# Pinning the issue order of three engines in a fused linear-attention and ReGLU kernel

## The chip, the cores and the metric

The kernel runs on one core of one Trainium2 chip. The metric is device time in microseconds (us), the median of several executions. One execution was also taken by the hardware profiler; times inside the kernel, such as "at 43.8 us", count from the start of its span. TensorE does matmuls, VectorE (DVE) and ScalarE (ACT) elementwise work, GpSimd (POOL) a few small operations, and SyncE (SP) issues nearly all DMA.

## The reference

The input `x` has 2048 tokens of 1024 values; weights and activations are bf16.

```python
phi = lambda t: jnp.where(t > 0, t + 1, jnp.exp(t)) + 1e-6
pq, pk = phi(q), phi(k)                      # 32 heads of 32, q, k, v = layernorm(x) @ wqkv
kv = einsum("bhsd,bhse->bhde", pk, v)
z = einsum("bhsd->bhd", pk)
o = einsum("bhqd,bhde->bhqe", pq, kv) / (einsum("bhqd,bhd->bhq", pq, z)[..., None] + 1e-6)
h = x + o.reshape(B, S, D) @ wo
n = layernorm(h)
gate, up = n @ W_gate, n @ W_up              # 1024 -> 3584
out = h + (gate * (gate > 0) * up) @ W_down  # 3584 -> 1024
```

## The kernel before

**Tiling.** Tokens go in 16 tiles of 128. Nearly every large product is done in the Strassen–Winograd way: both operands are split in two by two blocks, sums of blocks are formed (`left_sums` L113–123 for activations: L117 to L120; `right_ops` L127–138 for weights: L133 to L136; `weight_sums` L634–650 for gate and up: L642, L646, L647, L648), seven products replace eight, and their results are combined. Those sums and combinations are VectorE's work. `strassen` (L144–203) is the generator that does one product: matmuls into PSUM banks of tags A (two banks), D (one) and E (two); after products m1, u2 and u3, `snap` (L154) copies a PSUM bank to SBUF on ScalarE, so that TensorE may go on accumulating in the bank; and `fin` combines a bank with a copy.

**Stages.**
- *k and v, 0–122 us.* `ln_T` (L265) takes a token tile, forms its layernorm statistics on VectorE (L272, L275, and L287, which is mean times minus rstd), rstd on ScalarE (L277, L278), and the normalised tile `xn` on ScalarE (L288). The first tiles are transposed by TensorE (`transpose_in`, L299, copied out by L300), the others by a DMA. The first tiles then use plain products (`k_plain`, `v_plain`), later groups of four use `strassen` (`k_unit`, `v_unit`; matmuls L314, combinations L211 for k and L375 for v). phi of a result is finished by an exp on ScalarE (L216) and two operations on VectorE (L217, L218). `kv_tile` (L383) accumulates kv and z.
- *q, 122–206 us.* `q_unit` (L447, matmuls L454), with the same phi.
- *Attention, 146–270 us* (`attn_stages`, L513), in steps by tile with a lag between its parts: numerator and denominator in matmuls `nd` (L527) of 132 columns; 1/denominator on ScalarE as exp(−ln) (L531, L533); their product `o_sb` on VectorE (L534, two buffers); a transposing DMA to `oT` (L541); the `attn` matmuls with wo (L557); the residual sum on VectorE (L560); then the second layernorm (L572, L574–L578) to `hn`, another transposing DMA (L581) and its left sums.
- *Early gate and up products, 205–287 us* (`early_quad` L731, matmuls L738, combinations L747–L752), beside the second half of attention.
- *The rest, from 287 us:* gate and up products (`quad`, matmuls L851, copies L856, combinations L860–L864), then the down projection (L1171, L1345). Here `tc.manual_schedule` (L811) fixes the order of TensorE, VectorE and ScalarE as written.

**What sets the order.** Up to 287 us a scheduler decides in which order each engine's instructions are issued, from priorities (`tc.high_priority`), dependencies and its own estimate of when things are ready; a few edges are added by hand (`tc.issue_after`, and two `tc.add_manual_dep` at L793–798). Each engine then runs its instructions in that fixed order, and an instruction whose input is not there holds what is behind it. DMAs are issued by SyncE in SyncE's own order.

Of the kernel before, what the change touches and what calls it, by code (L numbers as in the profile page):

```python
# [19 lines left out]
def _load_act_set(nc, set_name="natural_log_exp_and_others"):  # L20
    from concourse.act_sets import SETS

    idx = [s.name for s in SETS].index(set_name)
    nc.scalar.add_instruction(
        mybir.InstLoadActFuncSet(
            name=nc.get_next_instruction_name(), act_func_set_id=idx, ins=[], outs=[]
        )
    )


@with_exitstack
def block_kernel(ctx: ExitStack, tc: tile.TileContext, x, wqkv, wo, wg, wu, wd, out, H: int):
    nc = tc.nc
# [19 lines left out]
    assert Dh == 32 and DW == NW and S % (4 * P) == 0 and FC % 4 == 0 and KC % 4 == 0  # L53

    _load_act_set(nc)

    consts = ctx.enter_context(tc.tile_pool(name="consts", bufs=1))
# [163 lines left out]
    order = [(i * HS + s * SW) // P + tt for s in range(NS) for i in range(2) for tt in range(NT)]  # L221
# [573 lines left out]
    for t, copy in ((order[-2], ("m1", 1)), (order[-1], ("u3", 1))):  # L795
        tc.add_manual_dep(squared[t].ins, quad_copies[2][copy].ins.name,
                          mybir.DependencyInfo(mybir.DependencyClass.NoSync, mybir.DependencyReason.DATA),
                          reason="order")
    ectx.close()
    pqctx.close()  # L800
    psctx.close()
# [220 lines left out]
    for r, (wt, f, fi, toks) in enumerate(runs):  # L1022
# [3 lines left out]
        for n, s in enumerate(toks):  # L1026
            first = n == 0 and grouped and fi == 0
# [502 lines left out]
@with_exitstack  # L1530
def kernel(
    ctx: ExitStack,
    tc: tile.TileContext,
    A_x: bass.AP,
    A_wqkv: bass.AP,
    A_wo: bass.AP,
    B_x: bass.AP,
    B_W_gate: bass.AP,
    B_W_up: bass.AP,
    B_W_down: bass.AP,  # L1540
    out: bass.AP,
):
    block_kernel(tc, A_x, A_wqkv, A_wo, B_W_gate, B_W_up, B_W_down, out, H=32)
# [30 lines left out]
```

## Time and profile before

| | us |
|---|---|
| median of 5 runs (lowest, highest) | 735.89 (735.41, 736.92) |
| the profiled execution | 735.41 |
| its span | 733.6 |
| first matmul of the hand-ordered part (accA, L851) | 287.3 |
| TensorE, VectorE, ScalarE busy in the span | 720.4, 580.4, 323.8 |

The span is what the profile covers; 1.8 us of the execution lie around it. In the list of waits a row reads: engine, the tile and line that waited, the engine, tile and line that it waited for, then total us, number of waits and the longest. In a timeline a row reads: start, length, engine, line, operation, tiles, sizes, and in brackets the idle time just before it with what ended that. In a table by stretches of time each engine has its busy us and its number of instructions; the granted TensorE clock (1.00 is full speed), the share of the 16 DMA engines' time that was busy, and GB/s stand last. "A <- B" reads: A is written from B, or A waits for B.

### The profile page before, as it was taken

To read this page: it belongs to the slowest core of one execution; us is meant where nothing else is said; L and a number is where in the kernel's file an instruction comes from. 1 tells how busy PE (TensorE), PEld (TensorE's weight loads), DVE (VectorE), ACT (ScalarE), POOL (GpSimd) and SP (SyncE) were. 2 spreads that over 40 slices of the span, in tenths; PEclk is the share of its full clock that TensorE was granted. 3 is DMA by queue.
4 is the path that set the end of the run, shared out by engine and by line. 5 is a ranking of instruction groups with operands and counts; after the bars stand their busy time and mean duration, and the time that the engine had idled before them with its cause. 6 is when DMAs were issued, how large, how long until landed. Compare 5 with 4: busy or idle time off the path is not lost.

```text
span 733.6 us, 10630 instructions
## 1 busy us (share of the span) xinstructions
PE 720.4 (98%) x4000; PEld 379.6 (52%) x4000; DVE 580.4 (79%) x1039; ACT 323.8 (44%) x580; POOL 20.7 (3%) x56
## 2 busy tenths in 40 slices
PE   7999999999999999999999999999999999999997
PEld 3444555444444444444444444444444468888566
DVE  6997644676789767789998998988987379996677
ACT  4876553778886655444344444444444120000000
POOL 1000000000000000000000000000000001100210
PEclk9999999999999999999999999999999999999999
DMA  9765002169976524177557576565553499977932
GB/s 314 166 150 159 1 1 76 41 150 224 236 167 172 136 73 136 44 226 222 162 169 238 204 231 229 172 201 171 181 179 120 142 396 332 313 258 276 257 45 58
DMA packets 144708, 128.89 MB, mean 176 GB/s; under 512 B 50960, under 2 KB 127888, under 8 KB 144656
## 3 DMA queue, kind: packets, MB, share of 16 engines
q1 hardware_dynamic: 137584, 123.30, 55.5%
q0 software_dynamic: 5312, 3.15, 3.6%
q10 hardware_dynamic: 1760, 1.77, 0.7%
q8 instruction: 31, 0.51, 0.3%
q14 instruction: 21, 0.17, 0.1%
HBM read 76.81 MB, written 39.85 MB: 159 GB/s over the span
## 4 chain that ended last, share of the span: by engine, by line
PE 81%; DVE 8%; DMA 5%; ACT 4%; issue 1%; SPq 0%; DVEq 0%; POOL 0%; ACTq 0%
PE accA L851 21%; PE accA L1345 8%; PE attn L557 6%; PE accX L851 6%; PE accY L851 5%; PE Aq L314 3%; PE Aq L738 3%; PE accA L1171 3%; PE accX L1345 3%; PE Aq L454 3%; PE accY L1345 2%; PE accA L939 2%; PE Eq L314 2%; PE accY L1171 2%; PE accX L1171 2%; PE Eq L738 2%
## 5 line engine op out<-in xcount | busy, mean ns | idle before, releaser
L856 ACT COPY snap<-accA 128x1024 f32<-128x1024 f32 x52 | 52.4, 1010 | 65.9 <-PE accA L851 65.7
L861 ACT ACTIVATE gu<-gu 128x512 bf16<-128x512 bf16 x72 | 45.4, 630 | 80.4 <-DVE gu L860 80.3
L851 PEld LDWEIGHTS <-tg 128*128 128x128 f16 x384 | 37.6, 98 | 45.4 <-issue 0.2
L851 PEld LDWEIGHTS <-tu 128*128 128x128 f16 x384 | 37.6, 98 | 45.3
L557 PE MATMUL attn<-wo_mem,oT 128*128 128x512 bf16 x256 | 58.6, 379 | 1.5 <-DVE o_sb L534 1.3
L851 PE MATMUL accA<-hn,tg 128*128 128x512 f16 (+1 forms) x192 | 49.3, 379 | 0.0
L851 PE MATMUL accA<-hn,tu 128*128 128x512 f16 (+1 forms) x192 | 49.3, 379 | 0.0
L154 ACT COPY u<-Aq 128x512 f32<-128x512 f32 x54 | 31.4, 583 | 36.8 <-PE Aq L314 19.4
L1345 PEld LDWEIGHTS <-x 128*128 128x128 f16 (+1 forms) x448 | 43.8, 98 | 5.5
L557 PEld LDWEIGHTS <-oT 128*128 128x128 bf16 x256 | 24.6, 97 | 31.9 <-issue 3.5
L860 DVE TENSOR_TENSOR gu<-accX,snap 128x1024 bf16<-128x1024 f32 x26 | 31.7, 1219 | 10.2 <-ACT snap L856 7.9
L860 DVE TENSOR_TENSOR gu<-accY,snap 128x1024 bf16<-128x1024 f32 x26 | 31.7, 1218 | 7.7 <-ACT snap L856 7.7
L851 PEld LDWEIGHTS <-wg 128*128 128x128 bf16 x208 | 20.3, 98 | 25.8 <-issue 1.3
L851 PEld LDWEIGHTS <-wu 128*128 128x128 bf16 x208 | 20.4, 98 | 24.5
L314 PEld LDWEIGHTS <-xT 128*128 128x128 bf16 (+1 forms) x192 | 18.6, 98 | 23.7 <-issue 2.3
L534 DVE TENSOR_TENSOR o_sb<-nd,rd 128x384 bf16<-128x384 f32 (+1 forms) x48 | 23.3, 507 | 8.3 <-ACT rd L533 6.1
L1309 POOL DMA_DIRECT2D out_dram<-o x12 | 15.2, 1265 | 505.0 <-DVE o L1305 503.2
L1345 PEld LDWEIGHTS <-xs 128*128 128x128 f16 x280 | 27.4, 98 | 3.2
L560 DVE SCALAR_TENSOR_TENSOR x_res<-attn,x_res 128x512 bf16<-128x512 f32 x32 | 21.9, 686 | 8.6 <-PE attn L557 8.4
L1351 DVE TENSOR_TENSOR snap<-accA,u 128x1024 f32<-128x1024 f32 x16 | 19.5, 1220 | 11.5 <-PE accA L1345 11.4
L864 DVE TENSOR_TENSOR hq<-gu 128x512 bf16<-128x512 bf16 x48 | 20.2, 421 | 10.0 <-ACT gu L861 9.8
L1171 PEld LDWEIGHTS <-x 128*128 128x128 bf16 (+1 forms) x168 | 16.4, 98 | 19.6
(268 smaller groups left out, 1508.8 us busy)
## 6 DMA issues: line engine op xcount, KB each, us to landing
x<-x_dram SPq DMA_DIRECT2D x17, 896.0 KB, 8.7
x_dram<-hq SPq DMA_DIRECT2D x28, 512.0 KB, 3.0
wg<-in_B_W_gate_dram SPq DMA_DIRECT2D x14, 512.0 KB, 4.6
wu<-in_B_W_up_dram SPq DMA_DIRECT2D x14, 512.0 KB, 5.9
x_dram<-hq SPq DMA_DIRECT2D x28, 256.0 KB, 2.4
wraw<-in_B_W_down_dram SPq DMA_DIRECT2D x14, 512.0 KB, 4.2
t_dram<-wt SPq DMA_DIRECT2D x21, 256.0 KB, 2.2
xd<-x_dram SPq DMA_DIRECT2D x6, 896.0 KB, 7.0
```

The costliest lines, as they stand in the source:

```text
L154: copies[nm, v] = nc.scalar.copy(out=snaps[nm, v], in_=bank[v][:])
L314: nc.tensor.matmul(ps[:], lhsT=left[m - 1][:, kc, r + v * P:r + (v + 1) * P], rhs=right[m - 1][:, kc, :], start=(start and kc == 0), stop= ...
L454: nc.tensor.matmul(ps[:], lhsT=rq[m - 1][:, kc, (c + v) * P:(c + v + 1) * P], rhs=left[m - 1][:, kc, :], start=(start and kc == 0), stop=( ...
L534: nc.vector.tensor_tensor(out=ov[:, c0:c0 + n], in0=ndv[:, :, 0:P].rearrange("p k (h e) -> p k h e", h=HPC), in1=rd[:, 0:n, :].unsqueeze(3 ...
L557: nc.tensor.matmul(ps[:], lhsT=st["oT"][:, c, :], rhs=wo_sb[:, c, j * NW:(j + 1) * NW], start=(c == 0), stop=(c == KC - 1))
L738: nc.tensor.matmul(ps[:], lhsT=w(v, m)[:, kc, :], rhs=left[m - 1][:, kc, :], start=(start and kc == 0), stop=(kc == KH - 1), skip_group_ch ...
L851: nc.tensor.matmul(ps[:, v, :], lhsT=w[v][n - 1][:, kc, :], rhs=left[n - 1][:, kc, :], start=(t is not None and kc == 0), stop=(kc == KH - ...
L856: nc.scalar.copy(out=st[nm][:], in_=halves(st["A"]))
L860: add(out=g[:], in0=halves(st[nm]), in1=st[base][:], op=ALU.add)
L861: nc.scalar.activation(out=g[:, 0, :], in_=g[:, 0, :], func=ACT.Relu)
L1171: nc.tensor.matmul(ps[:, t * NW:(t + 1) * NW], lhsT=x_tile(n, s, kh)[:, f, (t0 + t) * P:(t0 + t + 1) * P], rhs=w_tile(n, kh)[:, f, :], sta ...
L1345: nc.tensor.matmul(pv[:, tt, :], lhsT=left(m)[:, f, tt * P:(tt + 1) * P], rhs=right(m)[:, f, :], start=(t is not None and f == 0 and tt % ...
```

## The change

The kernel gets a table, `ISSUE_ORDER`, with one entry for each engine, and a loop at the end of the early gate/up stage. The loop collects the instructions of each engine that were emitted so far, in program order; the table's words ("start*length", a run of program-order numbers) say in which order they shall be issued; and between each instruction and the next in that order an edge of class `NoSync` is added. Such an edge binds the scheduler and adds neither a semaphore nor an instruction.

The order of issue that follows was listed for both kernels, engine by engine. The instructions are the same, and so are the orders of SyncE and GpSimd. TensorE's order differs in 30 places, VectorE's in 54, ScalarE's in 26, nearly all of them one or a few instructions moved past a few others, and none after 287 us. The moves that are spoken of below, by the time at which TensorE started the matmul concerned in the profile before:

| at us | what is moved |
|---|---|
| 16.6–20.2 | L287 of the third tile ahead of two L272 and a sum; L300 and an L288 (ahead of the exp L349) forward |
| 40.5–49.8 | copies L154 and a v copy ahead of the L288 that they followed; L211 ahead of L135 and L136 |
| 59.6 | L375 ahead of an L211 and L218s; a copy of u2 one place back |
| 60–80 | sums L117, L119, L120 of other units moved from the 40–60 us stretch to here |
| 72.5 | L211 ahead of L134 and of the L117 before it moved back |
| 151–157 | nd matmuls placed otherwise between the q products; an L534 ahead of other work on VectorE |
| 171–206 | L533 ahead of an L216 and an L578; L534 ahead of L218 |
| 211–216 | L216 ahead of L154 copies, which go back; L534 and L560 forward |
| 218–220 | tg's L646 ahead of three hn sums (L118–L120); tu's L642 forward |
| 228–230 | u copies L154 ahead of L531, L577, L578 |

```diff
+ISSUE_ORDER = {
+    "PE": """
+        0*24 32*4 40*3 24*4 36*4 28*4 43*5 56*12 48*4 68*4 52*4 80*4 88*4 72*4 84*4 92*3 76*4 95*121 232 216*16 233*44
...
+    "DVE": """
+        0*6 7*3 6 10 58 11 16*2 12 18 13 19 25*3 59 28 20 14*2 21 61 23*2 29 22 34*2 30 36 31*2 37 42*2 33 44 46 45 47
...
+    "Activation": """
+        0*3 4*3 3 8 7 10*2 9 12 14 16*3 15 13 20 19 21*5 27*2 26 29*2 32*3 31 37*2 35 39 46 36 47*2 51 54 52 40 55 53
...
+}
...
         tc.add_manual_dep(squared[t].ins, quad_copies[2][copy].ins.name,
                           mybir.DependencyInfo(mybir.DependencyClass.NoSync, mybir.DependencyReason.DATA),
                           reason="order")
+    emitted = {}
+    for ins in nc.cur_bb.bb.instructions:
+        if "PoolBoundary" not in type(ins).__name__:
+            emitted.setdefault(str(ins.engine).split(".")[-1], []).append(ins)
+    for engine, words in ISSUE_ORDER.items():
+        seq = []
+        for word in words.split():
+            start, length = (word.split("*") + ["1"])[:2]
+            seq += emitted[engine][int(start):int(start) + int(length)]
+        assert len(seq) == len(emitted[engine])
+        for late, first in zip(seq[1:], seq):
+            tc.add_manual_dep(late, first.name,
+                              mybir.DependencyInfo(mybir.DependencyClass.NoSync, mybir.DependencyReason.DATA),
+                              reason="order")
     ectx.close()
```

More of the change, by code (lines that the diff above doesn't have):

```diff
@@ L28, in _load_act_set @@
     )
+ISSUE_ORDER = {
+    "PE": """
+        0*24 32*4 40*3 24*4 36*4 28*4 43*5 56*12 48*4 68*4 52*4 80*4 88*4 72*4 84*4 92*3 76*4 95*121 232 216*16 233*44
+        288*2 277*7 290*4 284*4 294*305 600*12 599 612*8 624 620*4 625*115 744*4 740*4 748*10 760*4 776*4 764*4 780*5
+        788 758*2 785 768 786*2 769*5 789*3 816 774*2 817*2 792*3 819 795*3 820 798*2 821*3 848*5 800*16 824*6 853*3
+        830*2 856*2 832*16 858*14 888*8 920*8 872*8 952*3 880*8 896*6 955*3 902*2 958*5 904*16 928*6 963*3 934*2 966*2
+        936*16 968*12 984*8 980*4 1016*3 992*22 1019*3 1014*2 1022*38 1064*5 1060*4 1069*6 1080 1088*4 1075*5 1081*7
+        1092*12 1112*2 1104*3 1114*4 1107*3 1118 1110*2 1119*13 1152*4 1132*4 1168*4 1156*4 1172*3 1160*3 1136*16
+        1163*5 1175*5 1200*9 1180*4 1209*4 1184*16 1213*19 1248*19 1232*16 1267*21 1304*8 1288*16 1312*160
+    """,
+    "DVE": """
+        0*6 7*3 6 10 58 11 16*2 12 18 13 19 25*3 59 28 20 14*2 21 61 23*2 29 22 34*2 30 36 31*2 37 42*2 33 44 46 45 47
+        38*3 48 50 41 49 51 60 52 62 53 63 68 64 69 72 65 70 73 78 74 79 71 54 80 55*3 75 92 106 93 81 66 94 107 112
+        108 113 95 114 98 109 76*2 67 99 115 100 116*3 86 82*2 122 84 89 119 85 123 96 124 87*2 90*2 125 166*2 97 169
+        102*2 101 168 104*2 170 138 110 171 139*3 111 172 120 173 121 130 126*2 133 128*2 131*2 134*4 142*8 154 150
+        157 151*3 155*2 158*8 174*15 192 189 193 190*2 194 196 195 197*5 206 202*2 207 204 210*2 216 208*2 205 212*4
+        217 220*2 218 222 219 232 223*5 233 228*2 234 230*2 235 244 238 245 236*2 239 241 240 246*2 242*2 248 260
+        249*6 261 255 257 256 262 258*2 263*2 268 265 269 266 271 270 267 272*4 277 276 280*2 278*2 283*3 282 288 291
+        286 289 287 290 292*8 306*4 303 300*2 304 302 305 310 320 324 313 311*2 314 316*2 315 321*2 326 318 325 328
+        319 323 327 329*2 334 356*3 331 360 332*2 335 361*2 336 363 343 337 344 387 389 338 359 345 340 339 388 341
+        346 342 391 347*2 392 349 390 393*2 364 350*6 365*3 373 368*2 374 370 375 383*2 371 385 372 386 416 376 417
+        377 418 378 419*2 379*2 421 381 422*2 401*2 382 403*2 395*4 412*4 399*2 405*7 424 427*4 425*2 431*7
+    """,
+    "Activation": """
+        0*3 4*3 3 8 7 10*2 9 12 14 16*3 15 13 20 19 21*5 27*2 26 29*2 32*3 31 37*2 35 39 46 36 47*2 51 54 52 40 55 53
+        41*2 59*2 43*2 56 45 61 49*2 78*2 57 83*2 58 80 62*4 85*3 68 66 69 88 67 71 91*2 70 93 72*6 81*2 89*2 94*41
+        136 135 137*2 140 139 141*6 148 147 149*2 152 154 153 155 158 151 159 166 156*2 160 162 161 167 163*3 169*6
+        168 191 180 182 181 183 175 192 176 184 177 185 178*2 193*2 186 195 187 197 188 198 189*2 196 199 201 200 202
+        220 208*2 211 210 221 212*3 203 233 204*4 222*4 234 215*2 226 217 235 218 227 219 236 228 237 229 239 230 241
+        231 240 232 242 238 243*2 250 252 251 253 245 254 246 255 247*3 256 262 257 264 258 263 259 261 265*3 260
+        273*3 268*3 278 271*2 279*5 276*2 289*2 284 291*2 285 293*2 286*3 300 302 301 295 303 296 304 297 305 298*2
+        312 311 313 306 325 307 314 308 315 327 316*2 309 318 310 326 319 328 320 329 321 330 322 332 323 341 324 342
+        331 333*2 343*2 335 345 336*5 346*2 357 348*3 359 351 358 360 352*5 361 367*2 362 369*2 363 371 364*3 377 379
+        372 378 373 380 374*3 381*3 385 384 386*2 389 388 390*2
+    """,
+    "SP": """
+        0*9 10 12 14 16 18 9 20 11 22 13 26 15 28 17 30 19 32 21 36 23 27 40 29 24*2 31 33 44 34*2 37*3 42*2 41 46*3
+        50 45 51 53 55 52 49 56*3 61 54 62 59 63*2 60 67*2 70 73 65 69 66 71 74*2 72 78 76 80 82 77 79 84 86 81 83 87
+        85 88 90 93 95 92 89 91 100 103 96 99 94 97*2 106 109 105 101*2 104 114 117 113 107 110 108 111 121 112 115*2
+        118 125 119*2 122*2 127 124 126 128*3
+    """,
+    "Pool": """
+        0 3 1*2 4*15 21*5 19*2 26*15
+    """,
+}
```

## The prediction

> **What bounds the kernel.** First the busy times and their 40 slices of 18.3 us:
>
> ```profile
> PE 720.4 (98%) x4000; PEld 379.6 (52%) x4000; DVE 580.4 (79%) x1039; ACT 323.8 (44%) x580; POOL 20.7 (3%) x56
> ...
> DVE  6997644676789767789998998988987379996677
> ...
> PEclk9999999999999999999999999999999999999999
> ```
>
> TensorE is the bound; VectorE fills up in slices 3 (37–55 us) and from 200 us on. The sum of instructions is the same before and after (same rows on each engine in the order listing), so only waiting of TensorE can go. The list of TensorE's waits:
>
> ```profile
> PE tp L299 <- DVE xT L300: 2.7, 1, 2.7
> PE attn L557 <- DVE o_sb L534: 1.3, 4, 0.5
> ...
> PE accY L851 <- DVE gu L860: 1.1, 1, 1.1
> PE Dq L314 <- DVE wo_mem L211: 0.6, 1, 0.6
> PE nd L527 <- DVE o_sb L534: 0.5, 1, 0.5
> PE Aq L314 <- ACT m L154: 0.5, 1, 0.5
> PE Aq L738 <- DVE tg L646: 0.4, 1, 0.4
> PE Aq L314 <- ACT u L154: 0.3, 1, 0.3
> ```
>
> 2.7 lies at 9.3 us, ahead of every moved instruction that it needs; 1.1 lies at 336.9 us in the hand-ordered part. Idle time understates a late start, because the modelled end of a matmul (0.38 us long) overlaps the next. So I took, for each matmul in the trace, its start less the one before it, less the usual step (216 ns for 512 columns, 58 ns for nd's 132). Up to 290 us that adds up to 13.7 us, 4.5 of it before 10 us. **9.2 us is all the change can win**; 29 starts that are over 0.07 us late hold 8.75 of it, and the steps below go through them by their time.
>
> The Trainium skill (Perfetto Trace Analysis, Identifying the Most-Contended Engine) says that matmul busy share is no measure of headroom, and Optimization Strategy there sends one to the gaps on that engine. Here the waits from 10 to 290 us add up to 4.0 us of idle time (the rows above without tp and accY, and two of 0.2 not shown); priced by those gaps the change could win at most 4.0 us, so the page's warning holds against its own advice.
>
> **How the table acts.** It adds ordering edges without semaphores; each engine keeps its instructions and gets another order at 30 places of TensorE, 54 of VectorE, 26 of ScalarE. SyncE's and GpSimd's orders are unchanged, so no DMA issue is moved; DMAs shift only with producers. Nothing after 287 us changes order. Typical cases, from the timeline of TensorE, ScalarE and VectorE:
>
> ```profile
> 43.76 1.02 PE L314 MATMUL Aq<-pq_mem,xS 128*128 128x512 f16 x4 [0.47 <-ACT m L154]
> 44.89 1.02 PE L314 MATMUL Dq<-pq_mem,xT 128*128 128x512 bf16 x4
> ```
> ```profile
> 42.00 1.24 ACT L288 ACTIVATE xn<-x_sb,sma 128x1024 bf16<-128x1024 bf16 x1 [0.21 <-DVE sma L287]
> 43.15 0.56 ACT L154 COPY m<-Aq 128x512 f32<-128x512 f32 x1
> ```
> ```profile
> 41.88 1.22 DVE L135 TENSOR_TENSOR wv_sb<-wv_sb 128x2048 f16<-128x2048 bf16 x1
> 43.02 1.22 DVE L136 TENSOR_TENSOR tv<-wv_sb,tv 128x2048 f16<-128x2048 bf16 x1
> 44.15 0.68 DVE L211 SCALAR_TENSOR_TENSOR wo_mem<-Dq,m 128x512 bf16<-128x512 f32 x1
> ```
>
> The PSUM copy (L154) that frees TensorE's bank sits behind a normalisation (L288) whose result TensorE doesn't need for many us; L211 sits behind two weight sums of 1.22 us. In the new order both stand ahead of those. A copy is 0.57 us, so it ends near 42.3, before TensorE's need at 43.1: the whole 0.63 us lateness of 43.76 goes, likewise the 0.27 of 44.89.
>
> **Stage k, v (10–122 us)**, by place: gain.
> - 16.6, 18.0, 20.2: L287 ahead of the next statistics (two of 0.68), so L288 starts earlier; xT copy L300 and an L288 move up: 0.17 + 0.31 + 0.17 = 0.65.
> - 40.5: copies no longer behind L288: 0.10. 43.76 and 44.89: 0.63 + 0.27 = 0.90.
> - 49.75: u copy (49.13) behind an L288 that itself waited 1.38 us for L287; moved ahead: 0.49.
> - 59.6: L375 moved ahead (0.23), but a u copy put one 0.57 us copy later makes TensorE wait 0.30: −0.07.
> - 72.45: L211 (71.72) stood behind L134 (70.58, 1.22), which stands behind an L117 that waits for a transposing DMA; L211 goes ahead: 0.80. 121.2: 0.18.
>
> Sum 3.05. Nothing is made to wait that didn't, but a mover can find its input late and hold its queue: the three L211s that now follow the L117 waiting for the transpose that lands at 46.7 have 1.0 us of room each, so this costs nothing while that landing stays within 1 us of its place; beyond it, it costs TensorE us for us. Work moved back must be paid for:
>
> ```profile
> 40.00:60.00 20.00, 19.03 (x110) 9.33 (x109) 20.00 (x41) 16.41 (x30) 0.68 (x5) 1.00 0.50 102
> 60.00:80.00 20.00, 19.36 (x90) 8.70 (x89) 14.77 (x22) 10.53 (x19) 0.18 (x1) 1.00 0.52 145
> ```
>
> VectorE (third pair) is full in the first stretch and has 5.2 us free in the second. What is put off there are sums of operands (L120 needed at 78.5 us, L117 and L119 at 122 us); that cover is why I cost them at nothing. Without it each put-off 0.68 us sum would return as lateness; four of them are 2.7 us.
>
> **Attention and early gate/up (146–287 us).**
> - 151.5: 0.16 gone, nd's new wait for L218 of 0.19: 0.
> - 156.7: L534 starts at 152.2 in place of 152.8, the oT transpose (lands 155.98) follows it, its wo matmul: 0.63.
> - 171.1, 173.6: rd (L533) ahead of an L216 of 1.14 us gains 0.36; the next wait grows by 0.19: 0.17.
> - 194.7, 205.3: L534 ahead of L218; copies: 0.22. 162.0, 182.7, 189.5, 240.2 and 217.5 keep their causes: 0.
> - 211.3, 212.4, 216.4: L216 (209.05) moved ahead of L575–L578, L560 and L534 earlier: 0.40 + 0.48 of 0.64 + 0.12 = 1.00.
> - 218.9, 219.9: tg L646 (218.47) waits behind three hn sums (0.42 each); ahead, and tu moved up: 0.55 of 0.61, + 0.13 = 0.68.
> - 228.4, 229.4: u copies ahead of L577, L578, less 0.20 new: 0.15. 249.3: 0.03.
>
> ```profile
> 218.47 0.41 DVE L646 TENSOR_TENSOR tg<-wg,tg 128x512 f16<-128x512 bf16 x1
> ```
> ```profile
> 218.94 1.04 PE L738 MATMUL Aq<-hs,tg 128*128 128x512 f16 x4 [0.44 <-DVE tg L646]
> ```
>
> Sum 2.88; with 3.05, 5.9 us. Cover from 200 us on is thin:
>
> ```profile
> 200.00:230.00 30.00, 28.80 (x154) 13.23 (x152) 26.81 (x72) 24.16 (x68) 0.00 (x0) 1.00 0.77 171
> ```
>
> VectorE has 3.2 us free there; the 1.7 us won can be had only out of that.
>
> **What the trace doesn't show.** How neighbours overlap in the new order: VectorE starts its next instruction about 0.08 us before the end of the last where nothing waits (43.02 + 1.22 against 44.15), and not where a DMA or engine is late. Over some dozen places where it is full this is −1.0 to +1.0 us. Thirteen places keep less than 0.1 us of margin by my working; at 0 to 0.1 us each, 0 to 1.3 us. I give back 0.5 in all, nearer the small end, as most rows around them have a VectorE with idle gaps. **Gain 5.4 us.** The point where the hand-ordered part begins (first accA, 287.3 us) shifts whole: VectorE has idle gaps of 1.6–2.3 us at 265, 268, 284 and 291, so nothing there holds the old time.
>
> The profiled execution took 735.41 (span 733.6 and 1.8 around it), 0.48 below the median of 735.89. 735.41 − 5.4 = 730.0; as a median **730.5 us**.
>
> The skill also says (TensorE: Matmul & The Clock Gate, A second HAM failure mode) that many micro-idles can make the clock oscillate. The profile grants 1.00 through all of these gaps, so by the row the clock adds nothing; by the page there would be more to win than 9.2.
>
> **Rivals.**
> 1. *The waits refill.* The transposes and loads that gate L117 (landing 69.5 us) and oT don't land earlier, so 72.45 keeps 0.4–0.8 and 156.7 its 0.63; the full VectorE of 22–60 us hands 1 us back, and 200–230 gives 0.6. Gain 5.4 − 0.6 − 0.63 − 1.0 − 0.6 = 2.6: 733.3. For: TensorE follows VectorE closely where that is 20.00 of 20. Against: 5 us free after 60.
> 2. *Nothing to measure.* The scheduler's old order is moved, but each wait is replaced by the next in line: 735–737. For: 29 small stalls with different releasers. Against: the list names instructions that stood behind work not needed for many us.
> 3. *Slower: late oT.* In 150–200 us the DMA share is 0.98 and oT lands 0.73 us ahead of its matmul both at 156.7 and 162.0. If reordered L534s or nd's make one tile's transpose miss, the two o_sb buffers carry it on: each of 8 tiles loses the 0.73 margin's worth, 5.8 us, and the 3.05 of the first stage remains won: 735.9 + 2.7 = 738.6. It decides once L534 ends over 0.7 us later than now in a step. Against: L534 moves ahead, not back, in the steps I followed; later tiles have 5–8 us of room.
>
> **Chances.** Forecast (728.5–732) 0.62; rival 1 (732–734.4) 0.19; rival 2 0.08; rival 3 0.08; better than 728.5, 0.03. The range 728.5 to 734.4 holds 0.81: below by half of the rest of 9.2 us and the +1.0, above to rival 1 with the 1.3 us of lost margins. About 0.2% (1.5 us) is what a measurement can tell from no change: faster 0.84, same 0.08, slower 0.08.
>
> **What would show it.** Right: the waits on m and u L154, L211, tg L646 gone; matmuls at 60 us some 2 us earlier; VectorE's 60–80 us over 16 busy; first accA near 282; the 446 us behind it unchanged, with the 1.06 us wait on gu. Wrong: an L117 or L134 still ahead of late TensorE, attn waiting longer on o_sb than 1.3 us, or new waits in 20–60.

## The result, and the profile after

| | median, us (lowest, highest) | ratio to before, 95% interval |
|---|---|---|
| before | 735.86 (735.13, 738.05; 42 runs) | |
| changed kernel | 733.67 (731.89, 736.65; 22 runs) | 0.9971 [0.9964, 0.9978] |

The change wins 2.2 us. The forecast was 5.4 (730.5 us); the range, 728.5 to 734.4, holds the time, but 3.2 us of the gain that was worked out are missing. The profiled execution took 733.28 us with a span of 731.5.

Line numbers of the changed kernel are 49 higher than before's up to line 798 of before, and 63 higher behind that; those of the experiments are 50 or 51 higher than before's. So L154, L211, L117, L133 of before are L203, L260, L166, L182 below. The page of the changed kernel, busy times and slices:

```profile
PE 718.8 (98%) x4000; PEld 380.2 (52%) x4000; DVE 582.8 (80%) x1039; ACT 325.3 (44%) x580; POOL 21.0 (3%) x56
...
DVE  6998744686799777789998998988987379996677
...
PEclk9999999999999999999999999999999999999999
```

TensorE's waits in the changed kernel (who waited, for whom; us in total, times, longest; the wait for xT lies at 9 us, ahead of the moves, and its matmul starts only 0.08 us earlier than before):

```profile
PE tp L348 <- DVE xT L349: 2.1, 1, 2.1
PE Dq L363 <- DVE wo_mem L260: 1.9, 1, 1.9
PE attn L606 <- DVE o_sb L583: 1.2, 3, 0.6
...
PE accY L914 <- DVE gu L923: 1.1, 1, 1.1
PE Eq L363 <- DVE wo_mem L260: 0.7, 1, 0.7
PE Aq L363 <- ACT u L203: 0.3, 1, 0.3
```

Most of the waits that the prediction wanted gone are gone: the copy of m, tg, nd on o_sb. One has grown, from 0.6 to 1.9 us: TensorE's Dq for the combination L260. One is new: Eq for L260, 0.7. Both are in the k, v stage. Matched matmul by matmul, the changed kernel stands against before like this:

| matmul (start before, us) | start in the changed kernel | shift |
|---|---|---|
| 49.75 | 47.51 | −2.24 |
| 51.47 | 50.12 | −1.35 |
| 72.45 | 72.90 | +0.45 |
| 121.16 | 121.52 | +0.36 |
| 156.71 | 156.56 | −0.15 |
| 173.57 | 173.78 | +0.21 |
| 194.72 | 194.77 | +0.05 |
| 226.49 | 224.55 | −1.94 |
| 287.30 (first accA) | 285.16 | −2.14 |

Up to 48 us the moves win all that the prediction had for them. Then 0.9 us is lost at one matmul and 1.8 more by the second place (1.3 there, 0.5 on the way), so that the k, v stage ends 0.4 us later than before. The attention stage wins 2.5, and the hand-ordered part carries it to the end: 446.3 us in both.

The two places, TensorE and then VectorE, in the changed kernel's timelines:

```profile
50.12 1.89 PE L363 MATMUL Eq<-pq_mem,xS 128*128 128x512 bf16 x8 [0.72 <-DVE wo_mem L260]
...
72.90 1.02 PE L363 MATMUL Dq<-pq_mem,xT 128*128 128x512 bf16 x4 [1.93 <-DVE wo_mem L260]
```
```profile
46.95 0.20 DVE L323 BATCH_NORM_AGGREGATE mv<-stats 128x2 f32<-128x12 f32 x1
48.70 0.69 DVE L166 TENSOR_TENSOR xS<-xT 128x1024 f16<-128x1024 bf16 x1 [1.56 <-DMA xT<-xn]
49.31 0.15 DVE L336 SCALAR_TENSOR_TENSOR sma<-mv,sma 128x1 f32<-128x1 f32 x1
49.38 1.28 DVE L260 SCALAR_TENSOR_TENSOR wo_mem<-Eq,u 128x512 bf16<-128x512 f32 x2
```
```profile
69.70 1.22 DVE L182 TENSOR_TENSOR tq<-wq_sb 128x2048 f16<-128x2048 bf16 x1 [2.32 <-DMA wq_sb<-in_A_wqkv_dram]
71.55 0.69 DVE L166 TENSOR_TENSOR xS<-xT 128x1024 f16<-128x1024 bf16 x1 [0.63 <-DMA xT<-xn]
72.16 0.68 DVE L260 SCALAR_TENSOR_TENSOR wo_mem<-Dq,m 128x512 bf16<-128x512 f32 x1
```

In both, VectorE stands idle (the brackets) in front of a sum L166 or L182 whose operand a DMA has not yet landed, and the combination L260 that TensorE waits for stands behind that sum with its own inputs there for 2 to 3 us (e2 and e3 below run it without that sum ahead). VectorE's 20 us stretches say the same: where it was full, it now has idle time, and the next stretch is fuller but TensorE less busy.

```profile
40.00:60.00 20.00, 19.23 (x113) 9.58 (x111) 18.34 (x36) 16.51 (x26) 0.50 (x4) 1.00 0.47 101
60.00:80.00 20.00, 17.79 (x82) 7.83 (x81) 16.83 (x26) 9.81 (x17) 0.96 (x2) 1.00 0.53 145
```

### The profile page after: what moved, and what is told of

Read it like the earlier page. It is cut to its first block, busy times and chain, and to the rows that moved or that the text cites. A ratio compares the mean times of both kernels' runs of the same rounds, so it can differ in the third digit from the quotient of the medians.

```text
span 731.5 us, 10633 instructions
## 1 busy us (share of the span) xinstructions
PE 718.8 (98%) x4000; PEld 380.2 (52%) x4000; DVE 582.8 (80%) x1039; ACT 325.3 (44%) x580; POOL 21.0 (3%) x56
## 3 DMA queue, kind: packets, MB, share of 16 engines
q10 hardware_dynamic: 1760, 1.77, 0.7%
## 4 chain that ended last, share of the span: by engine, by line
PE 82%; DVE 7%; ACT 6%; DMA 3%; issue 2%; SPq 0%; DVEq 0%; ACTq 0%
PE accA L914 21%; PE accA L1408 8%; PE attn L606 6%; PE accX L914 6%; PE accY L914 5%; PE Aq L363 4%; PE accA L1234 3%; PE Aq L787 3%; PE accX L1408 3%; PE Aq L503 3%; PE accY L1408 3%; PE accA L1002 2%; PE Eq L363 2%; DMA xT<-xn 2%; PE Eq L787 2%; PE accX L1234 2%
## 5 line engine op out<-in xcount | busy, mean ns | idle before, releaser
L914 PE MATMUL accA<-hn,tu 128*128 128x512 f16 (+1 forms) x192 | 49.3, 379 | 0.0
L914 PE MATMUL accA<-hn,tg 128*128 128x512 f16 (+1 forms) x192 | 49.3, 379 | 0.0
L203 ACT COPY u<-Aq 128x512 f32<-128x512 f32 x54 | 31.2, 580 | 37.4 <-PE Aq L363 20.7
L583 DVE TENSOR_TENSOR o_sb<-nd,rd 128x384 bf16<-128x384 f32 (+1 forms) x48 | 23.6, 508 | 6.9 <-ACT rd L582 5.4
L927 DVE TENSOR_TENSOR hq<-gu 128x512 bf16<-128x512 bf16 x48 | 20.2, 421 | 10.0 <-ACT gu L924 9.8
```

What stands on the lines that cost most here:

```text
L203: copies[nm, v] = nc.scalar.copy(out=snaps[nm, v], in_=bank[v][:])
L583: nc.vector.tensor_tensor(out=ov[:, c0:c0 + n], in0=ndv[:, :, 0:P].rearrange("p k (h e) -> p k h e", h=HPC), in1=rd[:, 0:n, :].unsqueeze(3 ...
L914: nc.tensor.matmul(ps[:, v, :], lhsT=w[v][n - 1][:, kc, :], rhs=left[n - 1][:, kc, :], start=(t is not None and kc == 0), stop=(kc == KH - ...
```

## The experiments

Theory 1: the new order leaves sums that wait for a DMA at the head of VectorE's queue, with TensorE's combinations behind them; move the sums and the loss goes, whenever the DMA lands. Theory 2: the loss is the lateness of the transposing DMAs (48.6 in place of 46.7 us, 71.5 in place of 69.5), caused by loads just ahead of them on the queue. Theory 3: TensorE follows VectorE so closely that each stall which is taken away only appears at the next instruction. Edits are given as moves in an engine's order of issue; each was made in the table.

| kernel | median, us | before beside it | ratio, 95% interval |
|---|---|---|---|
| e1 attention moves only | 732.79 | 735.70 | 0.9961 [0.9949, 0.9973] |
| e8 k, v moves only | 736.13 | 735.41 | 1.0007 [0.9998, 1.0016] |
| e2 one waiting sum back | 732.60 | 735.70 | 0.9960 [0.9948, 0.9972] |
| e3 one combination forward | 733.13 | 735.70 | 0.9966 [0.9956, 0.9976] |
| e4 x_res load behind the transpose | 731.87 | 735.70 | 0.9958 [0.9945, 0.9971] |
| e5 e4 + eight sums back, in a block | 732.67 | 735.41 | 0.9956 [0.9944, 0.9969] |
| e6 e4 + wq loads behind the transposes | 730.48 | 735.41 | 0.9926 [0.9913, 0.9938] |
| e9 VectorE's sums back, spread | 729.92 | 735.25 | 0.9927 [0.9915, 0.9940] |
| e7 e5 + three attention stalls | 732.48 | 735.41 | 0.9953 [0.9939, 0.9966] |
| e10 all of it | 729.33 | 735.25 | 0.9918 [0.9905, 0.9932] |
| e11 12 warm-up matmuls | 733.68 | 735.54 | 0.9967 [0.9954, 0.9979] |
| e12 before, 19 warm-up matmuls | 735.25 | 735.54 | 0.9997 [0.9988, 1.0006] |

**Which half won: e1 and e8.** The table was cut at 135 us, where no engine's order differs. e1 keeps before's order ahead of the cut and the table's behind it; e8 is the reverse.

> The table's order from 135 us on (attention, early gate/up), the order of before ahead of it. Profile after: matmuls of 121 us come 0.4 us later than before, those of 250 us 2.1 earlier, so the k and v moves lost 0.4 and the attention moves won 2.5. Theory 1 and 2 (the k/v part is worth nothing as it stands, because a sum that waits for a transposing DMA holds VectorE's queue, or because the transpose itself lands late): 733.4 us, within 0.5 of the changed kernel. Rival (the one profiled execution misleads, the k/v moves do win most times): 734.5 or more.

> The complement of e1: the table's order up to 135 us, the order of before behind it. If the parts add up (e1 is 2.9 under before, the changed kernel 2.2), the k and v moves cost 0.4 to 0.9: 736.3 to 736.8 us, and with a wider spread than before has, since their stall depends on when DMAs land. Forecast of the prediction for this part alone: 732.8.

e1 took 732.79 us: 0.9961, or 2.9 us under before, and a little better than the whole change. e8 took 736.13: 1.0007, no gain. So the one profile did not mislead: the k, v moves win nothing as they stand (they change the time by −0.1 to +1.2 us, by e8's interval; the forecast had them at −3.05), the attention moves win what was forecast (2.88). e1 lies 0.6 below its expectation, e8 0.2.

**Moving one waiting sum: e2.** VectorE's order at 47 to 51 us:

```diff
 L323 mv<-stats
-L166 xS<-xT
 L336 sma<-mv,sma
 L260 wo_mem<-Eq,u
 L260 wo_mem<-Eq,u
 L260 wo_mem<-Dq,m
+L166 xS<-xT
 L167 xS<-xS,xT
```

> The changed kernel, with one VectorE instruction moved back: the sum L166 of 48.7 us, which waits for the transpose that lands at 48.6, goes behind the mean L336 and the three L260 that stand behind it. Theory 1 (head of the queue): the 0.88 us lateness at 50.1 goes, L336 and so the next transposes come some 1.5 us earlier, and part of the 2.1 us at 72.9 with them: 731.8 to 732.8 us. Theory 2 (the transpose's lateness): it still lands at 48.6, and sums needed later cost the same: 733.0 to 733.7. Theory 3 (each stall only hands over to the next): 733.7.

732.60 us. In its timeline the transpose still lands late (48.54) and VectorE no longer cares; the mean L336, the head of the next transposes' chain, runs at 47.0 and not at 49.3:

```profile
46.99 0.10 DVE L337 SCALAR_TENSOR_TENSOR sma<-mv,sma 128x1 f32<-128x1 f32 x1
47.37 0.69 DVE L261 SCALAR_TENSOR_TENSOR wo_mem<-Eq,u 128x512 bf16<-128x512 f32 x1 [0.27 <-ACT u L204]
48.23 0.69 DVE L261 SCALAR_TENSOR_TENSOR wo_mem<-Eq,u 128x512 bf16<-128x512 f32 x1 [0.17 <-ACT u L204]
48.84 0.68 DVE L261 SCALAR_TENSOR_TENSOR wo_mem<-Dq,m 128x512 bf16<-128x512 f32 x1
49.44 0.68 DVE L167 TENSOR_TENSOR xS<-xT 128x1024 f16<-128x1024 bf16 x1
```

TensorE's lateness at 50.1 is gone. Dq's, at 72, is then 2.45: TensorE arrives earlier at the same late sum. Theory 1 at the first place; theory 3 where nothing was done about the second.

**Letting one combination past: e3.** At 69 to 73 us:

```diff
+L260 wo_mem<-Dq,m
 L182 tq<-wq_sb
 L166 xS<-xT
-L260 wo_mem<-Dq,m
 L183 tq<-wq_sb,tq
```

> The changed kernel, with one VectorE instruction moved forward: the combination L260 of 72.2 us goes ahead of L182, which waits for the wq load, and of L166, which waits for the transpose that lands at 71.5. Theory 1: its inputs are there at 69.3, so the 2.1 us lateness at 72.9 shrinks to 0 to 0.3: 731.5 to 732.0 us. Theory 3: the next L260, behind the same L182 and L166, is late instead, 1 to 2 us: 733 to 733.7.

733.13 us, the rival's figure. The 2.1 us lateness at 72.9 went and 1.42 and 0.87 came at 78 and 80, for the next two L260, which still stood behind sums of the eight. In the profiled execution it also cost something unforeseen. In its table of stretches TensorE's granted clock (third from the end) falls:

```profile
76.00:78.00 2.00, 0.91 (x5) 0.29 (x3) 2.00 (x3) 0.69 (x1) 0.00 (x0) 1.00 0.00 0
78.00:80.00 2.00, 1.13 (x5) 0.48 (x5) 2.00 (x4) 1.76 (x3) 0.00 (x0) 1.00 0.00 0
80.00:82.00 2.00, 2.00 (x10) 1.06 (x9) 1.88 (x4) 1.57 (x2) 0.00 (x0) 0.54 0.00 0
82.00:84.00 2.00, 2.00 (x24) 2.00 (x23) 1.93 (x5) 1.31 (x2) 0.45 (x2) 0.61 0.00 0
84.00:86.00 2.00, 2.00 (x17) 1.05 (x15) 1.52 (x3) 1.11 (x2) 0.25 (x2) 1.00 0.00 0
```

After two idle gaps, 1.25 and 0.71 us, inside 3.4 us the clock was halved for 3.41 us (80.14 to 83.56 in the trace's clock record), which costs about half of that, 1.7 us by estimate. That execution took 734.91 us, 1.8 over the median; of the twelve on record only one other has a mean granted clock below 0.999 (736.26 us, 0.998). So the median of 733.13 doesn't hold this loss, and theory 3 doesn't need it.

**The loads ahead of the transposes: e4 and e6.** e4 moves one issue on SyncE:

```diff
-L594 x_res<-in_A_x_dram
 L339 xT<-xn
+L594 x_res<-in_A_x_dram
```

> The changed kernel, with one DMA issue moved: the x_res load issued at 43.0 us goes behind the transpose issued at 43.6. Theory 2 (a transpose waits for the load issued just ahead of it): the transpose lands 3.0 to 3.4 us after its issue, near 46.8, not 48.6, VectorE's L166 is not late, and the result is 731.8 to 732.8 us. If the load has no part in it, the landing stays at 48.6 and the time at 733.7.

731.87 us, and the transpose lands at 46.92, 3.27 us after its issue: it looks like theory 2 confirmed. It was not: e5 and e7 have the same edit, and their transpose took 4.80 and 4.92 us again. What the load ahead costs is about 0.3 us (the last of the transpose's data packets ends 2.67 us after issue in e4, 2.98 in the changed kernel). The rest is told under e11.

e6 takes e4, puts the two wq loads behind the last two transposes, and moves the four sums of wq back to 85 us; L166 stays at the head.

```diff
-L295 wq_sb<-in_A_wqkv_dram
-L295 wq_sb<-in_A_wqkv_dram
 L339 xT<-xn
 L339 xT<-xn
+L295 wq_sb<-in_A_wqkv_dram
+L295 wq_sb<-in_A_wqkv_dram
```

> e4, with the two wq loads issued behind the last two transposes, and only the wq sums (L133 to L136 in before's lines) put back to 85 us; the sum L117 stays ahead of the combination at 70.3. Theory 2 (the transposes are late because they queue behind the loads just ahead): they land 3 to 4 us after issue, at 64 to 66 us, not 68.7 and 69.6; L117 is then free at the head and the 1.6 us at 71.0 goes: 730.1 to 730.7 us. If the loads have no part in it, the transposes still land after 68 and the time is e4's, 731.9.

730.48 us. SyncE's own timeline, first of the changed kernel, then of e6:

```profile
61.90 0.38 SPq L295 DMA_DIRECT2D wq_sb<-in_A_wqkv_dram  x1
62.38 7.03 SPq L339 DMA_TRANSPOSE xT<-xn  x2
```
```profile
58.34 4.80 SPq L340 DMA_TRANSPOSE xT<-xn  x2
63.24 1.21 SPq L296 DMA_DIRECT2D wq_sb<-in_A_wqkv_dram  x2
```

Behind the loads of 1 MB each the two transposes occupy SyncE's queue for 7.03 us and land 8.3 and 4.6 us after issue, at 70.7 and 71.5. Ahead of the loads each one issues in 1.23 us and lands 3.0 and 3.2 us after issue, at 61.4 and 65.1. Here theory 2 holds for the transposes: L166 at 66.67 waits for nothing, and none of the lateness in 50 to 122 us is over 0.2 us (steps doubled by a matmul that the trace lacks left out). But e6 moves four of VectorE's sums too, and no run moves the loads alone.

**VectorE alone: e5 and e9.** e5 is e4 with all eight sums (L166 to L169, L182 to L185) in one block behind the stage's combinations.

> e4 (x_res load behind the transpose), and VectorE's eight sums of 67.7 to 79 us that wait for the wq loads and the last transposes (L117 to L120 and L133 to L136 in before's lines; needed from 95 us on) go behind the last combination of that stage, near 85 us. Theory 1 (a waiting sum at the head of VectorE's queue holds the combinations): the 1.6 us lateness at 71.0 goes and none of its size takes its place (e3, which let only one combination past, got 1.4 and 0.9 us at 78 and 80): 1.4 to 1.8 under e4's 731.9, so 730.1 to 730.5 us. Theory 3 (each stall hands over): 731.5 or more.

A miss: 732.67. The lateness at 71 went, but I had built a new one: the four sums of 1.22 us now ran from 86.65 to 91.31 us in front of the L425s that TensorE's next Eq, due at 90.7, waited for, and Eq came 1.93 us late at 92.65:

```profile
90.18 1.22 DVE L186 TENSOR_TENSOR tq<-wq_sb,tq 128x2048 f16<-128x2048 bf16 x1
91.31 0.68 DVE L425 TENSOR_TENSOR v_sb<-Dq,m 128x512 bf16<-128x512 f32 x1
```

And at 50.0 us a late transpose (48.5) held the same sum once more, as e5 does not have e2's move. e9 has it, spreads the sums into VectorE's gaps, and leaves all DMA issues where the changed kernel has them:

```diff
-L182 tq<-wq_sb
-L166 xS<-xT
 L260 wo_mem<-Dq,m
...
 L424 v_sb<-Dq,m
+L166 xS<-xT
+L167 xS<-xS,xT
+L168 xT<-xT,xT
+L169 xS<-xT,xS
 L424 v_sb<-Dq,m
+L182 tq<-wq_sb
 L424 v_sb<-Eq,u
 L424 v_sb<-Eq,u
+L183 tq<-wq_sb,tq
...
```

> The changed kernel with VectorE's order alone altered, DMA issues as they were: the waiting sum of 48.7 us goes behind the mean and the three combinations (as in e2), and the eight sums that wait for the wq loads and the last transposes (e5) go behind the stage's combinations, this time spread (four of 0.68 us at 85, the four of 1.22 us one at a time, at 89, 93, 96 and 98 us), as e5 lost 1.9 us at 92.7 by setting them in one block. Theory 1 (VectorE's queue is held by a waiting sum; the late transposes themselves cost nothing once nothing stands behind them): 2.4 under e2's 732.6, so 730.0 to 730.5 us, with the transposes still landing after 69 us. Theory 2 in its strong form (the late landing decides): 732 or more.

729.92 us (five runs from 729.90 to 729.94), 0.9927 [0.9915, 0.9940]: 5.3 us under before. The transposes and loads land as late as ever (48.3, 70.2 and 71.1 us), and TensorE waits for none of it. All its waits in e9:

```profile
PE tp L350 <- DVE xT L351: 1.5, 1, 1.5
PE spin L451 <- DVE zero L448: 1.2, 1, 1.2
PE accY L916 <- DVE gu L925: 1.1, 1, 1.1
PE attn L608 <- DVE o_sb L585: 1.0, 2, 0.6
PE Aq L365 <- ACT u L205: 0.3, 1, 0.3
PE tp L350 <- ACT xT L351: 0.2, 1, 0.2
```

This settles theory 1 for the k, v stage: 3.75 us between the changed kernel and e9 hang on where nine sums of VectorE stand, with the DMA side untouched. e6 reaches nearly the same end with five of the nine left in place and their transposes on time, and its four wq sums moved back; what the place of the loads alone is worth stays open.

**The attention stalls that the table leaves: e7, e10.** On ScalarE four instructions of 1/denominator (L580, L582) go ahead of the normalisation L627 and the exp L265 at 170 us, two ahead of L627 at 245; on VectorE the products o_sb (L583) ahead of L266.

> e5, and in the attention part three of the stalls left by the table: 1/denominator (ScalarE) ahead of the hn and exp that hold it, and o_sb (VectorE) ahead of L217, at 170 to 173 us (0.80 late in the changed kernel); the same ahead of hn at 245 us (0.54); a copy of e5 ahead of a Square at 188 us (0.26). Theory 1 (work that waits or isn't yet needed at the head of a queue): 1.3 to 1.6 under e5, so 728.7 to 729.1 us. Theory 3: less than 0.5 under e5.

732.48 us, 0.2 under e5, not 1.3. In its trace the lateness of 173.8 (0.80) and 247 (0.54) is gone, but 0.31 is new at 176 (a residual sum behind L267, L268, which are L266 and L267 of the changed kernel) and 0.71 at 191, which came with a PSUM copy that was moved forward as well (its tile is called e5; it is not the run e5). That was theory 3 at work. e10 leaves that copy alone and moves two residual sums too:

> e9 and e6 together (sums back and spread, x_res and wq loads behind the transposes), and in the attention part 1/denominator and o_sb ahead of hn, exp and L217 at 170 to 173 us (0.80 late in the changed kernel), two residual sums ahead of L217 and L218 there (e7 got 0.3 of new lateness from them), and 1/denominator ahead of hn at 245 us (0.54). The e5 copy moved in e7 stays where it was, as 0.7 us at 191 came with it. Theory 1: 1.0 to 1.4 under e6's 730.5, so 729.1 to 729.5 us. Theory 3 (each stall hands over to the next): 730.2 or more.

729.33 us, 0.9918 [0.9905, 0.9932], 5.9 us under before: 1.15 under e6 and 0.6 under e9. Of the attention waits none of over 0.1 us on o_sb is left:

```profile
PE accY L916 <- DVE gu L925: 1.1, 1, 1.1
PE Aq L365 <- ACT u L205: 0.3, 1, 0.3
PE Aq L789 <- DVE hh L803: 0.2, 1, 0.2
```

It beats both kernels. The last row is a new stall at 270 us (0.36 late).

**Why the first transpose was late: e11 and e12.** In the DMA records one packet of 16 KB belongs to the instruction queue (q8), about every 25 us. In the changed kernel it starts at 46.34 us and lasts 1.18; the transpose's data packets end at 46.59, but the last packet of 4 bytes of the 32 that close it goes only at 47.51, and the landing follows 1.1 us later. The DMA view of the changed kernel from 46.2 to 47.6 us (queue, packets, MB, share of 16 engines) has that packet:

```profile
q1 hardware_dynamic: 241, 0.05, 18.2%
q8 instruction: 1, 0.02, 5.3%
```

Across the kernels (us; the closing packets are the last of that transpose):

| kernel | transpose issued | 16 KB packet starts | last closing packet | landed, after issue |
|---|---|---|---|---|
| before | 43.27 | 46.41 | 46.24 | 3.44 |
| e4 | 43.65 | 46.33 | 46.32 | 3.27 |
| e6 | 44.31 | 46.84 | 46.88 | 3.12 |
| e10 | 44.05 | 46.72 | 46.72 | 3.18 |
| e1 | 44.19 | 47.45 | 46.79 | 3.08 |
| changed | 43.61 | 46.34 | 47.51 | 5.00 |
| e2 | 43.54 | 46.31 | 47.45 | 5.00 |
| e3 | 43.51 | 46.45 | 47.32 | 5.00 |
| e8 | 43.61 | 46.36 | 47.50 | 4.98 |
| e9 | 43.49 | 46.26 | 47.24 | 4.84 |

Where the closing packets are out by the time that packet starts (within 0.04 us), the transpose takes 3.1 to 3.4 us; where they are not, 4.8 to 5.0. Before missed it by 0.17 us. e5 and e7 fit: 30 of the 32 closing packets are out by 46.29 and 46.57, the 16 KB packet starts at 46.49 and 46.88, the last two go after 47.2 and 47.5. Two kernels were to move the packet by altering the number of warm-up matmuls alone (`SPIN = 16`).

```diff
-    SPIN = 16
+    SPIN = 12
```

> The changed kernel with 12 warm-up matmuls (spin) in place of 16, nothing else altered: TensorE is 8 instructions further on at each time after the start, so that the 16 KB packet of the instruction queue that goes out at 46.3 us in the changed kernel goes out some 0.9 us later, while the transpose's last packets (46.3 to 46.6) stay. Theory 2b (the transpose lands at 48.6 and not near 47 because its last packet stands behind that packet on one DMA engine): it lands at 46.9 to 47.1, VectorE's wait of 1.56 us goes, and with it the 0.88 us lateness at 50.1: 0.7 to 1.9 under the changed kernel's 733.7, so 731.8 to 733.0 us. If the x_res load ahead of it is the cause: still 48.6 and 733.7.

The packet moved further than expected, to 49.73, and the transpose landed 3.37 us after its issue, with the x_res load still ahead of it. VectorE's L168 (before's L117) no longer waits:

```profile
48.14 0.20 DVE L325 BATCH_NORM_AGGREGATE mv<-stats 128x2 f32<-128x12 f32 x1
48.26 0.69 DVE L168 TENSOR_TENSOR xS<-xT 128x1024 f16<-128x1024 bf16 x1
```

So the landing is as expected and the 0.88 us lateness is gone, but the time is not: 733.68. The clock fell to half from 9.72 to 13.14 us (the trace's clock record), and what follows starts 1.2 us later than in the changed kernel; all five executions have a mean clock of 0.997 or 0.998. By 63 us the profiled execution has made that good, and its 732.60 us are 0.7 under the changed kernel's profile; but it is the fastest of the five, and where the others lose 1.1 us more at the median no profile shows.

The same trace holds a second case. Its 16 KB packet of 239.54 us starts 2.94 us after the issue of a transpose of hn (236.60 us), and that transpose lands after 5.03 us; the same transpose takes 3.2 to 3.6 us in the other thirteen traces, where no such packet meets it.

e12, the other way round on the kernel before (same order, `SPIN = 19`):

> The kernel before, same order, with 19 warm-up matmuls in place of 16: the packet of the instruction queue that goes out at 46.4 us, just behind the transpose's last packets (46.0 to 46.2), goes out near 45.8, ahead of them. Theory 2b: the transpose that landed at 46.7 lands at 47.3 to 48.3, VectorE's sum of 47.2 is up to 1.1 us late, and 0 to 0.7 us are lost: 735.4 to 736.5 us. Otherwise: it lands at 46.7 and the time is that of before.

It tells nothing: the packet stayed at 46.43 us, the transpose landed 3.33 us after issue, and the time (735.25, 0.9997) is that of before. What sets the moment of that packet stays open: four warm-up matmuls fewer moved it by 3.4 us, three more by 0.02. That a transpose which meets it lands some 1.6 us later stands on the table above and on the two cases of e11; no run moved the packet and nothing else.

## Why the prediction was wrong, point by point

- **The bound, 9.2 us of lateness up to 290 us, and the method of pricing by late starts**: borne out. e10 wins 5.9 us, more than the 4.0 that the idle gaps would have allowed, with few stalls over 0.3 us left.
- **k, v up to 48 us**: right, and nearly to the tenth. Forecast by then 0.65 + 0.10 + 0.90 + 0.49 = 2.14, measured 2.24.
- **"Nothing is made to wait that didn't ... the three L211s that now follow the L117 waiting for the transpose that lands at 46.7 have 1.0 us of room each, so this costs nothing while that landing stays within 1 us"**: this step failed, and it failed by its own condition. The landing came 1.9 us later, beyond the 1.0 of room, and cost 0.88 us at 50.1. The step took the landing from the profile of before as if it were fixed. It also left out the mean L287 that stands behind the same sum and heads the next transposes: it ran 1.5 us later, and some 0.7 us of that reached the last transpose (e2 runs the mean at 47.0, and that transpose lands at 70.80, not 71.46). The other 1.3 us of its lateness against before have no cause shown.
- **"72.45: ... L211 goes ahead: 0.80"**: this step failed worst. The move table above says that L211 went ahead of L134 and of L117; the profile after shows it ahead of L134 alone, still behind the L133 that waits for the wq load and the L117 that waits for the last transpose. So the stall was not taken away; with the landing 2.0 us later (69.46 to 71.46) it grew from 0.80 to 2.10: 0.80 was to be won, 1.29 were lost. Nor would the old landing have saved the term: in e4, with the same order on VectorE, the last transpose lands at 69.55 and the matmul is still 1.60 late, as TensorE gets there earlier. The prediction had also read the queue's head wrongly. It was not L117 that waited in the profile before, but L133, for the wq load:

```profile
67.64 1.22 DVE L133 TENSOR_TENSOR tq<-wq_sb 128x2048 f16<-128x2048 bf16 x1 [2.19 <-DMA wq_sb<-in_A_wqkv_dram]
68.78 1.28 DVE L375 TENSOR_TENSOR v_sb<-Eq,u 128x512 bf16<-128x512 f32 x2
69.98 0.68 DVE L117 TENSOR_TENSOR xS<-xT 128x1024 f16<-128x1024 bf16 x1
```

- **59.6**: a loss of 0.07 was forecast, 0.5 measured (0.22 late at 57.8, 0.44 at 61.2, 0.09 at 63.0, against 0.23 before). This too hangs on the first landing: where it is on time and the order the same (e4, e11), 0.17 to 0.18 is left. e2, e9 and e10, which move that sum back, have 0.18 and 0.48 here.
- **The cover, VectorE's 5.2 free us in 60–80 us**: the free time was there and the sums were put there, but a stretch's sum of free time says nothing on order: a sum in a free stretch costs nothing only where it does not wait. In e9 the eight sums run at 83 to 96 us instead; VectorE is then 12.14 us busy in 60–80 us, less than before, and TensorE 19.68.
- **Attention, 2.88**: right in size (2.5 in the trace, 2.9 in e1). In its terms: 156.7 and 211 to 230 as forecast; 171 to 173.6 not (forecast 0.17 gained, 0.34 lost: 0.80 late at 173.8, as 1/denominator came behind both the normalisation and the exp).
- **Hand-ordered part handed on whole**: right, 446.3 us in both.
- **Rival 1** gave 733.3 and is the case that came, but not by its own sum, so that its number and the range fit is partly luck: the landing did keep 72.45 and more, while 156.7 and 200 to 230 us paid in full. **Rivals 2 and 3**: excluded; oT landed in time.
- **The clock**: the prediction quoted a rule of the Trainium skill (TensorE: Matmul & The Clock Gate, A second HAM failure mode), that many micro-idles can make the clock oscillate, and set it aside, as before's profile grants 1.00 throughout. The changed kernel's profile does too, over a single gap of 1.93 us. e3's and e11's do not: 3.41 us at half clock in each. So the row was right for these two profiles, and the rule agrees with e3: stalls can cost more than their length. The changed kernel's other executions show it as well, without a trace: the four slowest on record (735.41 to 736.65 us) have a mean granted clock of 0.995 to 0.998, all others 0.999 or 1.000. That part of its spread the sum had no term for; without those four the median would be 0.2 us lower.

What the chances lacked: the k, v terms were added up as if independent, but those between 48 and 80 us hang on two landings. One look at what a landing 1 us later would do at each moved instruction would have shown the whole second half of that stage at risk.

## What to carry to other kernels

When an order of issue is pinned, go through each engine's queue for instructions that wait for a DMA, and ask what stands behind each one and for whom; a sum not needed for 20 us belongs behind the combinations that free a PSUM bank, even if its operand has always been in time by a little. Take a DMA's landing as an interval and not as a number, and issue a transposing DMA ahead of bulk loads, not behind them. Where VectorE has room, spread long operations into it one at a time; a block of them is a stall of its own.

## What the runs showed of the hardware

- Two transposing DMAs issued behind two loads of 1 MB held SyncE's queue for 7.03 us together and landed 8.3 and 4.6 us after issue (changed kernel); ahead of them each issued in 1.23 us and landed 3.0 and 3.2 us after (e6).
- Transposing DMAs met by a 16 KB packet of the instruction queue (one about every 25 us) ahead of their last closing packets took 4.8–5.0 us, not 3.1–3.4; 0.1 to 0.2 us in either's start decided.
- After two idle gaps of 1.25 and 0.71 us within 3.4 us TensorE's clock was half for 3.41 us (e3), and so it was after one of 2.48 us at 9.2 us (e11); one of 1.93 us (changed kernel), 1.77 (e5) or, at 9.8 us, 2.90 (e10) left it at 1.00. The length of a single gap doesn't decide it, and no run shows what does.
- The times spread over 0.04 us in five runs of e9, 0.8 in five of e10 and 4.8 in 22 of the changed kernel, whose slowest are those with the lower clock. That the waiting sums cause the spread isn't shown.
